# Retention and SwiGLU on one core: four edits to the order and placement of small work in the first batch and at the end

## The chip, the cores and the metric

The kernel runs on one NeuronCore of a Trainium2 chip. Its engines work in parallel, each through its own queue in order: TensorE (PE in the profile; its weight loads are listed apart as PEld), VectorE (DVE), ScalarE (ACT), GpSimd (POOL) and SyncE (SP), which here only issues DMAs. They meet through semaphores. The metric is the device time of one execution in microseconds (us).

## The reference

Eight batches of eight heads go through retention (attention with a decay instead of a softmax); the result, reordered to 4608 tokens of 512 values, goes through a SwiGLU feed-forward block.

```python
# q, k, v: (8, 8, 576, 64) float32; gamma one value per head
scores = scale * np.matmul(q, k.transpose(0, 1, 3, 2))
ret = scores * Dmat          # Dmat[h, i, j] = gamma[h] ** (i - j) for i >= j, else 0
attn = np.matmul(ret, v)
x = attn.transpose(0, 2, 1, 3).reshape(4608, 512)
g = x @ w_gate               # w_gate, w_val: (512, 1536)
val = x @ w_val
out = (g * sigmoid(g) * val) @ w_out      # w_out: (1536, 512)
```

## The kernel before, in words

The tokens are taken in five tiles: tile 0 of 512 tokens, and tiles 1 to 4 of 1024. Everything stays in SBUF; four PSUM banks, `bankA`, `bankB`, `bankC` and `bankE`, take the large matmuls in turn, and `inner` and `outer` hold the retention's.

**Retention.** Heads go in pairs, four pairs per batch. `tick(t)` runs three pairs in different phases at once: it loads and transposes pair t, computes scores and chunk states of pair t-1, and finishes pair t-2, whose values lie in `outer` (matmuls L531, L554, L558) and are copied with their decay into `x` by `to_x` (L646, L622). The next pair's L531 can begin only when those copies have read `outer`. The masks and scans between (L579 to L601) are VectorE's, copies and scalings mostly ScalarE's; from batch 1 on, q and k are transposed by VectorE (L489, into `qT` and `kT`).

**Weights.** The weights come from DRAM in half-blocks. `split(j)` (L404, L405, on ScalarE) takes a half-block's bits apart, and `rounding(j)` (L418, L419, on VectorE) makes the rounded float32 weight of it and calls the next `split`. Roundings 0 to 3 are the gate and value weights of the first two blocks of hidden columns, which `up0` (L747) multiplies in tile 0.

**Tile 0** is multiplied as it stands, `up0` and `down0`. **Tiles 1 to 4** use a bilinear scheme with 26 block products where a plain product has 32. The hidden columns are three quads of 512. For each quad, `up_step` runs 26 steps (the table `UP`); each step adds up a left operand from blocks of the weights and a right operand from blocks of `x`, multiplies them (L972, eight matmuls of 128x256), and adds its result into partial sums. `down_step` does the same 26 times per tile over all three quads (table `DOWN`, L1015, twelve matmuls). A row of `UP` has: the place of its bank in the rotation and whether its product starts a new sum; the slot of the `x` operand and the sums for it; the slot of the weight operand and the sums for it; and what is done with the product. Rows of importance here (steps 0-based):

```python
"3= | 12:  | 11: sub 8 11 6 | copy 6",                                  # step 3
"1= | 4: sub 13 0 2 | 10: nad 11 11 0 | add 2 b 2, neg 12 2",           # step 5
"0+ | 21: add 18 18 7 | 7: nad 9 1 3 | add 2 b 2, sub 4 4 2, add 5 5 4",# step 15
"1+ | 22:  | 8: sub 11 1 10 | add 2 b 2, neg 13 2",                     # step 16
"3= | 18: sub 23 1 3, sub 24 5 23 | 0: nad 6 6 12 | add 6 b 6",         # step 17
"0= | 7:  | 9: add 2 2 4 | add 1 b 1, add 3 b 3, neg 15 1, neg 3 3, add 6 6 3, neg 2 6",  # step 18
"2+ | 24: sub 1 1 5 | 11: sub 12 0 12 | add 3 b 3",                     # step 19
"2+ | 23: sub 25 7 24 | 12: nad 3 3 10 | add 7 b 4, out 1 7",           # step 22
```

In the last column `b` is the bank, numbers are partial sums ("parts", 128x512), `copy` is ScalarE's (L912), and `out` and `neg` end in a SiLU on ScalarE (L990) and a product of it with the value half (L993, L996, L997), which is put off by a step. In the weights' column, `nad d a b` is d = -(a + b): ScalarE negates a into d (L942), then GpSimd subtracts b (L943). Other weight sums are GpSimd's (L781).

In **tile 1** (`busy` in the code, the "first batch" of the change's name; 175.7 to 329.7 us of the span for its up-projection) the weight sums are made for the first time, in place, and each operand is stored to DRAM (L976, issued on ScalarE's queue); tiles 2 to 4 fetch them back (L876). A slot may be overwritten only when its matmul has read it and its store has landed. VectorE does the `x` sums and all sums of `reads` (L915) in this tile; in the others, GpSimd does those sums of `reads` that don't read a bank.

**The order of the work** is written out by hand: inside the manual schedule each engine runs its instructions in the order in which the program emits them. In `up_step`, that is: `x` sums, weight sums with their negations, the matmuls, the store of the weight operand, `reads`, and pieces of retention work (`part_on`) between. Results leave tile by tile: `down_step`'s `result` stores 256 tokens by 256 columns in one DMA (L1024) on SP.

Of the kernel before, what the change touches and what calls it, by code (L numbers as in the profile page):

```python
# [17 lines left out]
ALU = mybir.AluOpType  # L18
# [136 lines left out]
def kernel(  # L155
# [32 lines left out]
    nc = tc.nc  # L188
# [4 lines left out]
    P = 128  # L193
    HP = H // 2
# [7 lines left out]
    TB = TW // 4  # L202
# [4 lines left out]
    starts = list(range(T0 - TW, NT, TW))  # L207
# [465 lines left out]
    def tick(t, lo=HP, hi=NP, spread=False, then=None):  # L673
        go_on(len(pieces))
        if hi == HP:

            if lo <= t - 1 < hi:
                scores(t - 1, True)
                new_states(t - 1)
                pieces.extend(masked(t - 1))  # L680
                go_on(3)
            if lo <= t - 2 < hi:
                own_values(t - 2)
            for f in transposes(t) if lo <= t < hi else ():
                f()
            if t + 1 == HP:
                split(0)
                rounding(0)
            if lo <= t - 2 < hi:
                earlier_values(t - 2)  # L690
                to_x(t - 2)[0]()
            return
        if lo <= t - 2 < hi:
            own_values(t - 2)
        if lo <= t - 1 < hi:
            new_states(t - 1)
        if lo <= t - 2 < hi:
            earlier_values(t - 2)
        if lo <= t - 1 < hi:
            scores(t - 1, t - 2 < lo)  # L700
        if lo <= t - 1 < hi and whole(t - 2) and not whole(t - 1):
            decay(slice(0, H), slice(0, H), half[1])
        copies, *masks = masked(t - 1) if lo <= t - 1 < hi else (lambda: None,)
        keys, *new = transposes(t) if lo <= t < hi else (lambda: None,)
        outputs = to_x(t - 2)[0] if lo <= t - 2 < hi else lambda: None
        late = needed(1) - 4 <= t < needed(1) - 2 or light(t - 2)
        if late and masks:
            own, (pairs, odd, evens) = masks
            pieces.extend([lambda: (copies(), outputs(), own()), [pairs, odd, lambda: (evens(), keys())]])
        elif late:  # L710
            pieces.append(lambda: (copies(), outputs(), keys()))
        else:
            pieces.extend([lambda: (copies(), keys()), outputs])
            pieces.extend(masks)
        if then and new:
            pieces.extend(new[:-1])
            pieces.append(lambda: (new[-1](), then()))
        else:
            pieces.extend(new)
            pieces.extend([then] if then else [])  # L720
        if not spread:
            go_on(len(pieces))
# [176 lines left out]

    products = []  # L900

    def reads(ops, bank, busy, result):

        at = lambda a: bank if a == "b" else part[int(a)]
        old = len(products)
        for op in ops:
            if op[0] in ("copy", "add", "sub"):
                while any(a == op[1] for a, _ in products):
                    products.pop(0)[1]()
                    old -= 1  # L910
            if op[0] == "copy":
                nc.scalar.copy(out=at(op[1]), in_=bank)  # L912
            elif op[0] in ("add", "sub"):
                eng = nc.vector if "b" in op or busy else nc.gpsimd
                eng.tensor_tensor(out=at(op[1]), in0=at(op[2]), in1=at(op[3]),  # L915
                                  op=ALU.add if op[0] == "add" else ALU.subtract)
            else:
                product = result(int(op[1]), at(op[2]), op[0] == "neg", op[2] == "b" or busy)
                if product and op[2] == "b":
                    product()  # L920
                elif product:
                    products.append((op[2], product))
        for _ in range(old):
            products.pop(0)[1]()
# [5 lines left out]
    def x_sums(n, lo, hi, vector):  # L930
        for op in x_ops[lo:hi]:
            add(nc.vector if vector or op[0] == "nad" else nc.gpsimd, op, x_view(n))

    def w_sums(qd, i):
        view = up_view(qd)
        for op in up[i][5]:
            if op[0] == "nad":

                dst, a, b = [view(int(s)) for s in op[1:]]
                if op[3] == op[1]:  # L940
                    a, b = b, a
                nc.scalar.mul(out=dst, in_=a, mul=-1.0)  # L942
                nc.gpsimd.tensor_tensor(out=dst, in0=dst, in1=b, op=ALU.subtract)  # L943
            else:
                add(nc.gpsimd, op, view)
# [10 lines left out]
    def up_step(n, qd, i):  # L956
# [18 lines left out]
        if busy:  # L975
            nc.scalar.dma_start(out=up_ops[qd][i].rearrange("p (g x) -> p g x", g=2), in_=w)  # L976
            if i in (20, 23) and qd + 1 < NQ:
                first_sums(qd + 1, *((0, 2) if i == 20 else (2, 4)))
            if i == 24 and qd + 1 < NQ:
                w_sums(qd + 1, 1)  # L980
            if qd + 1 == NQ:
                for _ in range({21: 3, 22: 2, N - 1: 3}.get(i, 0)):
                    fetch()
        else:
            fetch()
# [10 lines left out]
                return lambda: nc.vector.tensor_tensor(out=dst, in0=src[:, TB : 2 * TB], in1=s, op=ALU.mult)  # L996
            nc.gpsimd.tensor_tensor(out=dst, in0=src[:, TB : 2 * TB], in1=s, op=ALU.mult)  # L997

        reads(ops, b, busy, result)
        if qd + 1 == NQ and i + 1 == N:  # L1000
            while products:
                products.pop(0)[1]()
# [3 lines left out]
    def down_step(n, i):  # L1006
        label, opens, slot, hops, ops = down[i]
        for op in hops:
            add(nc.gpsimd if i % 3 == 1 and op[0] != "nad" else nc.vector, op, hid_view)
        w = operand().rearrange("p (q x) -> p q x", q=NQ)  # L1010
        lhs = hid_view(slot)
        b = bank(label, i == 0)
        for qd in range(NQ):
            for m in range(2):
                nc.tensor.matmul(b[:, m * TB : (m + 1) * TB], lhs[:, qd, ts(m, P)], w[:, qd],  # L1015
                                 start=(opens and qd == 0 and m == 0), stop=(qd == NQ - 1), skip_group_check=True)
        fetch()

        def result(o, src, negative, vector):
            if negative:  # L1020
                nc.scalar.mul(out=src, in_=src, mul=-1.0)
            d, t = divmod(o, 4)
            rows = starts[n] + t * TB
            nc.sync.dma_start(out=out[rows : rows + TB, d * TB : (d + 1) * TB].rearrange("(m p) d -> p m d", p=P),  # L1024
                              in_=src.rearrange("p (m d) -> p m d", m=2))

        reads(ops, b, False, result)
        at = 2 * (i - (N - 1 - X_FIRST // 2))
        if 0 <= at < X_FIRST and n + 1 < NTILE:
            x_sums(n + 1, at, at + 2, True)  # L1030
        go_on(3)
# [10 lines left out]
    for t in range(HP + 2):  # L1042
        tick(t, 0, HP)

        if t == 3:
            load(HP)
        for j in {3: (1,), 4: (2, 3), 5: (4, 5)}.get(t, ()):
            rounding(j)
        for f in range(2):
            if t > 3:  # L1050
# [41 lines left out]
    for m, f in enumerate(down_order):  # L1092
# [6 lines left out]
            first_sums(0, 0, 1)  # L1099
        if m == 8:  # L1100
            first_sums(0, 1, 4)
            w_sums(0, 1)
        if m > 8:
            x_sums(1, 3 * (m - 9), min(3 * (m - 8), X_FIRST), True)
# [64 lines left out]
```

## Time and profile before

| | |
|---|---|
| Median of three runs | 1051.49 us (1051.44 to 1051.83) |
| Profiled execution | 1051.82 us |
| Its span, first to last instruction | 1050.1 us |
| TensorE busy | 1025.6 us, 98% |
| VectorE busy | 660.9 us, 63% |
| GpSimd busy | 393.1 us, 37% |
| ScalarE busy | 294.1 us, 28% |
| VectorE busy from 190 to 330 us | 107.84 of 140 us |
| GpSimd busy from 190 to 330 us | 82.97 of 140 us |
| ScalarE busy from 190 to 330 us | 55.21 of 140 us |

The profile is of one execution; times in its timelines count from the start of the span. A line of a timeline has the start, the duration, the engine, the line of the kernel, the operation, what it writes and reads, the shape, how often it came in a row, and in brackets how long the engine had been idle before it and what ended that. In the table of waits a line has the waiting engine with what it writes and its line, then the releaser, the total in us, the number of waits and the longest. A matmul that starts afresh after a wait is listed somewhat longer than one in a running stream. A sum that reads two operands in SBUF and one that reads a bank have the same line (L915) and differ by what stands after the arrow.

### The profile page before, as it was taken

How to read it: one execution, taken by the hardware profiler on the slowest of the kernel's cores; microseconds unless marked ns; L12 is line 12 of the kernel's file. 1: busy time of each engine (PE TensorE's matmuls, PEld its weight loads, DVE VectorE, ACT ScalarE, POOL GpSimd, SP SyncE). 2: the span in 40 equal slices, each digit the busy share in tenths (PEclk: the TensorE clock that was granted, in tenths of full speed). 3: DMA queues.
4: the chain of work that ended last, by engine and by line, in shares of the span. 5: the costliest groups of instructions: out<-in, count | busy, mean ns of one | idle time of the engine just before them, and what ended most of it. 6: DMA issues, size and time to landing. Idle time of an engine off the chain costs nothing.

```text
span 1050.1 us, 21509 instructions
## 1 busy us (share of the span) xinstructions
PE 1025.6 (98%) x8448; PEld 840.9 (80%) x8448; DVE 660.9 (63%) x1071; ACT 294.1 (28%) x646; POOL 393.1 (37%) x338
## 2 busy tenths in 40 slices
PE   6999999999899999999999999999999999999998
PEld 5444555888787888888888888888888888888887
DVE  5578878778779767554467787526376645344644
ACT  4376433242533322132322102223120022231110
POOL 2002367656365016622124048312250483222505
PEclk9999999999999999999999999999999999999999
DMA  9999768776678788755676777545554565555553
GB/s 243 246 281 278 183 193 271 197 202 183 173 201 228 234 192 261 198 147 172 185 203 160 229 176 226 152 141 151 152 180 137 155 195 156 151 152 161 180 162 98
DMA packets 310363, 199.09 MB, mean 190 GB/s; under 512 B 220152, under 2 KB 254968, under 8 KB 310264
## 3 DMA queue, kind: packets, MB, share of 16 engines
q1 hardware_dynamic: 279128, 161.65, 57.0%
q10 hardware_dynamic: 31136, 36.08, 10.3%
q8 instruction: 67, 1.10, 0.4%
q14 instruction: 32, 0.26, 0.1%
HBM read 157.56 MB, written 40.11 MB: 188 GB/s over the span
## 4 chain that ended last, share of the span: by engine, by line
PE 75%; DVE 5%; issue 1%; ACT 1%; DMA 1%; ACTq 0%; POOL 0%; DVEq 0%; SPq 0%
PE bankC L972 12%; PE bankE L972 12%; PE bankA L972 11%; PE bankB L972 11%; PE bankA L1015 6%; PE bankB L1015 6%; PE bankC L1015 6%; PE bankE L1015 6%; DVE rest L915 2%; PE outer L531 1%; DVE arena L993 1%; PE inner L572 1%; PE outer L558 1%; PE inner L542 1%; DVE rest L781 0%
## 5 line engine op out<-in xcount | busy, mean ns | idle before, releaser
L915 POOL TENSOR_TENSOR rest<-rest 128x512 f32<-128x512 f32 x56 | 79.4, 1423 | 293.1 <-DVE rest L915 274.6
L990 ACT ACTIVATE io<-rest 128x256 f32<-128x256 f32 x180 | 75.0, 417 | 338.2 <-DVE rest L915 289.8
L972 PE MATMUL bankC<-rest,arena 128*128 128x256 f32 x544 | 129.1, 380 | 0.5 <-DVE rest L915 0.5
L972 PE MATMUL bankA<-rest,arena 128*128 128x256 f32 x544 | 128.8, 380 | 0.0
L781 POOL TENSOR_TENSOR arena<-arena 128x512 f32<-128x512 f32 (+1 forms) x72 | 115.4, 1617 | 29.0 <-DMA up<-arena 20.9
L972 PE MATMUL bankE<-rest,arena 128*128 128x256 f32 x512 | 121.4, 380 | 2.5 <-DVE rest L915 2.5
L972 PE MATMUL bankB<-rest,arena 128*128 128x256 f32 x512 | 121.4, 380 | 0.8 <-POOL arena L943 0.8
L972 PEld LDWEIGHTS bankC<-rest,arena 128*128 128x128 f32 x544 | 102.9, 190 | 15.3 <-issue 0.9
L972 PEld LDWEIGHTS bankA<-rest,arena 128*128 128x128 f32 x544 | 103.1, 190 | 14.8 <-issue 0.8
L997 POOL TENSOR_TENSOR arena<-rest,io 128x256 f32<-128x256 f32 x72 | 51.9, 725 | 166.9 <-ACT io L990 166.9
L972 PEld LDWEIGHTS bankE<-rest,arena 128*128 128x128 f32 x512 | 96.9, 190 | 16.4 <-issue 2.3
L972 PEld LDWEIGHTS bankB<-rest,arena 128*128 128x128 f32 x512 | 97.0, 190 | 14.7 <-POOL arena L943 1.6
L781 POOL TENSOR_TENSOR rest<-rest 128x256 f32<-128x256 f32 (+1 forms) x66 | 67.5, 1044 | 102.2 <-DVE rest L419 61.7
L915 DVE TENSOR_TENSOR rest<-bankC,rest 128x512 f32<-128x512 f32 x72 | 48.7, 685 | 64.4 <-PE bankC L972 43.6
L915 DVE TENSOR_TENSOR rest<-bankB,rest 128x512 f32<-128x512 f32 x72 | 48.8, 686 | 63.7 <-PE bankB L972 44.8
L915 DVE TENSOR_TENSOR rest<-bankE,rest 128x512 f32<-128x512 f32 x72 | 48.8, 685 | 63.2 <-PE bankE L972 46.2
L915 DVE TENSOR_TENSOR rest<-bankA,rest 128x512 f32<-128x512 f32 x72 | 48.8, 686 | 62.8 <-PE bankA L972 45.5
L993 DVE SCALAR_TENSOR_TENSOR arena<-rest,io 128x256 f32<-128x256 f32 x84 | 58.5, 699 | 10.9 <-ACT io L990 10.9
L1015 PE MATMUL bankA<-arena 128*128 128x256 f32 x252 | 58.0, 380 | 1.3 <-DVE arena L781 1.3
L1015 PE MATMUL bankB<-arena 128*128 128x256 f32 x252 | 58.4, 382 | 0.0
L1015 PE MATMUL bankC<-arena 128*128 128x256 f32 x252 | 58.1, 380 | 0.0
L1015 PE MATMUL bankE<-arena 128*128 128x256 f32 x252 | 57.9, 379 | 0.0
(188 smaller groups left out, 1632.3 us busy)
## 6 DMA issues: line engine op xcount, KB each, us to landing
arena<-up SPq DMA_DIRECT2D x234, 256.0 KB, 2.7
arena<-dn SPq DMA_DIRECT2D x104, 384.0 KB, 3.6
up<-arena ACTq DMA_DIRECT2D x78, 256.0 KB, 3.2
dn<-rest SPq DMA_DIRECT2D x78, 128.0 KB, 1.8
out_dram<-rest SPq DMA_DIRECT2D x32, 256.0 KB
qk<-in_q_dram SPq DMA_DIRECT2D x108, 72.0 KB, 2.5
qk<-in_k_dram SPq DMA_DIRECT2D x108, 72.0 KB, 2.6
rest<-in_moe_w_out_dram ACTq DMA_DIRECT2D x6, 1024.0 KB
```

The lines of the kernel that those rows point to most:

```text
L531: m = nc.tensor.matmul(value(i, hl, c), s["v"][rows, at], ret[rows, c % 2 if whole(i) else hl, c // 2], start=start, stop=start, skip_grou ...
L542: nc.tensor.matmul(z[half[hl], r, c], s["kn"][chunk(i, hl, 2 * c + r, i < HP)], s["v"][rows, at], start=True, stop=True, skip_group_check= ...
L558: nc.tensor.matmul(xr[half[hl]] if c + 1 == NC else value(i, hl, c), state[half[hl], c, :], s["qT"][half[hl], column(i, hl, c)], start=Fal ...
L572: nc.tensor.matmul(sc[chunk(i, hl, 2 * c + r)[0], r if whole(i) else hl, c], kT[half[hl], at], qT[half[hl], at], start=True, stop=True, sk ...
L781: eng.tensor_tensor(out=dst, in0=srcs[0], in1=srcs[1], op=ALU.add if op[0] == "add" else ALU.subtract)
L915: eng.tensor_tensor(out=at(op[1]), in0=at(op[2]), in1=at(op[3]), op=ALU.add if op[0] == "add" else ALU.subtract)
L972: m = nc.tensor.matmul(b[:, gv * TB : (gv + 1) * TB], w[:, gv, ts(c, P)], rhs[:, c, :], start=(opens and gv == 0 and c == 0), stop=(c == 1 ...
L990: nc.scalar.activation(out=s, in_=src[:, 0:TB], func=AF.Silu, scale=-1.0 if negative else 1.0)
L993: return lambda: nc.vector.scalar_tensor_tensor(out=dst, in0=src[:, TB : 2 * TB], scalar=-1.0, in1=s, op0=ALU.mult, op1=ALU.mult)
L997: nc.gpsimd.tensor_tensor(out=dst, in0=src[:, TB : 2 * TB], in1=s, op=ALU.mult)
L1015: nc.tensor.matmul(b[:, m * TB : (m + 1) * TB], lhs[:, qd, ts(m, P)], w[:, qd], start=(opens and qd == 0 and m == 0), stop=(qd == NQ - 1), ...
```

## The change

There are four edits.

1. At the start, `tick(3)` emits `rounding(0)` after the output copies of pair 1 instead of before them, and `tick(4)` emits `rounding(2)` and `rounding(3)` before the output copies of pair 2; they were emitted after that tick.
2. In tile 1 the negation of a step's `nad` is emitted a step earlier by a new function `negated`: after the store of the step before and ahead of that step's `reads`.
3. In tile 1, from step 14 on, sums of `reads` that read no bank go to GpSimd instead of VectorE (`spread`).
4. The very last sum of the kernel and its store are split into two halves of 128 tokens, the second stored through ScalarE's queue.

```diff
 def tick(...)
             if t + 1 == HP:
                 split(0)
-                rounding(0)
             if lo <= t - 2 < hi:
                 earlier_values(t - 2)
+                if t == HP:
+                    rounding(2)
+                    rounding(3)
                 to_x(t - 2)[0]()
+            if t + 1 == HP:
+                rounding(0)
             return
...
-    def reads(ops, bank, busy, result):
+    def reads(ops, bank, busy, result, spread=False):
...
-                eng = nc.vector if "b" in op or busy else nc.gpsimd
+                eng = nc.vector if "b" in op or (busy and not spread) else nc.gpsimd
...
+    def negated(qd, i):
+
+        view = up_view(qd)
+        for op in up[i][5]:
+            if op[0] == "nad":
+                nc.scalar.mul(out=view(int(op[1])), in_=view(int(op[3] if op[3] == op[1] else op[2])), mul=-1.0)
+
     def w_sums(qd, i):
...
-                nc.scalar.mul(out=dst, in_=a, mul=-1.0)
                 nc.gpsimd.tensor_tensor(out=dst, in0=dst, in1=b, op=ALU.subtract)
...
             if i == 24 and qd + 1 < NQ:
+                negated(qd + 1, 1)
                 w_sums(qd + 1, 1)
+            if 0 < i < N - 1:
+                negated(qd, i + 1)
...
-        reads(ops, b, busy, result)
+        reads(ops, b, busy, result, i > N // 2)
...
+        if n + 1 == NTILE and i + 1 == N:
+            _, o, a = ops.pop()
+            d, t = divmod(int(o), 4)
+            at, rows = part[int(a)], starts[n] + t * TB
+            assert ops == [["add", a, "b", a]]
+            for m, queue in enumerate((nc.sync, nc.scalar)):
+                nc.vector.tensor_tensor(out=at[:, ts(m, TB)], in0=b[:, ts(m, TB)], in1=at[:, ts(m, TB)], op=ALU.add)
+                queue.dma_start(out=out[rows + m * P : rows + (m + 1) * P, d * TB : (d + 1) * TB], in_=at[:, ts(m, TB)])
+            return
...
-        for j in {3: (1,), 4: (2, 3), 5: (4, 5)}.get(t, ()):
+        for j in {3: (1,), 5: (4, 5)}.get(t, ()):
             rounding(j)
...
             first_sums(0, 1, 4)
+            negated(0, 1)
             w_sums(0, 1)
```

## The prediction

> **What bounds the kernel now.** I read the engine table first, then TensorE's waits, then the timelines around those waits.
>
> ```profile
> PE 1025.6 (98%) x8448; PEld 840.9 (80%) x8448; DVE 660.9 (63%) x1071; ACT 294.1 (28%) x646; POOL 393.1 (37%) x338
> ```
>
> TensorE (PE) works through 98% of the span: 24.5 us of idle is all that a change off TensorE can win, and only where it ends a wait. The waits, one line each (waiter, releaser, us, times, longest):
>
> ```profile
> PE outer L531 <- DVE rest L622: 2.6, 2, 2.3
> PE bankE L972 <- DVE rest L915: 2.5, 2, 1.9
> PE outer L566 <- DVE kT L489: 1.6, 1, 1.6
> PE bankB L972 <- POOL arena L943: 0.8, 2, 0.5
> PE bankC L972 <- DVE rest L915: 0.5, 1, 0.5
> ```
>
> All lie before 330 us, where the start (to 42 us) and tile 1's up-projection (175.7 to 329.7 us, three quads of 26 steps of 1.73 us) are. In the start, VectorE's timeline (start, duration, engine, line) and TensorE's show the 2.3 us wait:
>
> ```profile
> 22.70 0.43 DVE L418 TENSOR_SCALAR arena<-rest 128x512 int32<-128x512 int32 x1 [0.75 <-ACT rest L404]
> 23.29 0.69 DVE L419 CUSTOM_DVE_ANT_0 arena<-arena,rest 128x1024 uint16<-128x1024 uint16 x1 [0.16 <-ACT rest L405]
> ...
> 24.03 1.28 DVE L622 TENSOR_TENSOR rest<-outer,tab 128x256 f32<-128x256 f32 x3
> 25.70 0.46 PE L531 MATMUL outer<-ret,v 64*64 64x64 f32 x16 [2.29 <-DVE rest L622]
> ```
>
> Rounding 0 (L418, L419) stands in VectorE's queue ahead of the output copies (L622) that free PSUM's `outer` for TensorE.
>
> In the up-projection VectorE is the engine that runs late. Quad 1, steps 15 to 22, timelines of VectorE, GpSimd (POOL), ScalarE (ACT) and TensorE:
>
> ```profile
> 254.05 2.38 DVE L915 TENSOR_TENSOR rest<-rest 128x512 f32<-128x512 f32 x2
> 262.26 1.68 DVE L915 TENSOR_TENSOR rest<-rest 128x512 f32<-128x512 f32 x1
> 263.87 2.90 DVE L993 SCALAR_TENSOR_TENSOR arena<-rest,io 128x256 f32<-128x256 f32 x2
> 266.87 0.69 DVE L915 TENSOR_TENSOR rest<-bankE,rest 128x512 f32<-128x512 f32 x1
> 254.52 1.36 POOL L943 TENSOR_TENSOR arena<-arena 128x512 f32<-128x512 f32 x1 [6.30 <-ACT arena L942]
> 260.71 5.77 POOL L781 TENSOR_TENSOR arena<-arena 128x512 f32<-128x512 f32 x4
> 253.81 0.63 ACT L942 ACTIVATE arena<-arena 128x512 f32<-128x512 f32 x1 [0.60 <-DMA up<-arena]
> 267.70 1.96 PE L972 MATMUL bankE<-rest,arena 128*128 128x256 f32 x8 [1.93 <-DVE rest L915]
> ```
>
> The first two lines are the three sums that this change moves; step 22 waits 1.93 us for bank E, which the fourth line frees.
>
> [...]these 512-wide sums take 0.69 us alone (233.48) and 1.68 us beside GpSimd, while sums with a PSUM input stay at 0.69 us.[...]
>
> **The change part by part.**
>
> *Start: 1.4 us.* Rounding 0 goes behind the copies of head pair 1, roundings 2 and 3 ahead of those of pair 2; ScalarE's order stays. The copies need pair 1's matmuls, whose last (L558) end near 22.4, and VectorE is free at 21.96: they run 22.4 to 23.8 instead of 23.9 to 25.3. TensorE, ready at 23.4, goes on near 24.2 instead of 25.70: 1.5 us. Next late: rounding 0 now 23.8 to 25.1, for a matmul due at 25.7; rounding 1 to 26.3, due 27.5; masks 26.3 to 28.9; rounding 2 to 30.1, while bank C's matmul comes due at 29.2. It waited 0.85 us at 31.76 and starts near 30.3: 1.45 us. Rounding 3 ends at 31.3, due 32.1; copies of pair 2 end at 32.7, needed at 33.9. From 42 to 164 us TensorE has no wait. The weight roundings lead it by 5 us at 53 us, and the long run of stores on SP (69 from 131.50) begins behind loads of k and v whose buffers TensorE frees, so it shifts along. I take 1.4.
>
> *Negations: nothing by themselves, 0.3 us in quad 2.* Six weight sums per quad need a negation on ScalarE. Two keep their place in ScalarE's order (those of steps 1 and 7); those of steps 5, 15, 17 and 22 move ahead of the SiLU of the step before, which waited for VectorE. No instruction is added; one is 0.61 us. GpSimd's sums of steps 5, 17 and 22 are released some 1.5 to 4 us earlier. That ends the 0.3 us at 190.00 (step 8), but step 9 then waits for VectorE (0.56 us at 192.56), so nothing is won. In quad 2, step 25 waits 0.28 us for the sum at 326.56, released by a negation at 325.87; a step ahead it is done by 324: with its restart 0.3 us. What is queued behind: step 15's negation waits for the store of step 13 (landed 253.8), and now SiLU 14 stands behind it, 252.80 becoming some 254.4. VectorE's product of it comes only after step 15's sums, and its wait is under 1 us, where 2.4 us of sums are gone. Without that cover every us of late landing is a us of VectorE.
>
> *Sums to GpSimd: 1.2 us.* The queues show three per quad, nine in all, not four: two at step 15, one at step 18. VectorE loses 2.38 + 1.68 us in quad 1. GpSimd gains 3 x 1.27 = 3.8 us per quad, and its order ties it: step 16's `add 2 b 2` must wait until GpSimd has read part 2, and step 19's `add 3 b 3` until it has read part 3. Quad 1: sum of step 15's weights 254.5 to 255.8, VectorE's product to 256.15, the two moved sums to 258.7, then two weight sums and a VectorE product of 0.35 to 261.6 (step 20 needs the second at 262.16), `add 2 2 4` to 262.9, product to 263.25, moved sum to 264.5, product to 264.85, and bank E is read by 265.5 instead of 267.5. Step 21 ends at 265.6: the 1.93 us wait is gone. But GpSimd, idle from 266.5 to 271.9 before, now still has three sums to do until 270.3, and they cost VectorE some 0.6 us at a product and 0.9 at the small scans (L596). So `kT` (L489), for which TensorE waited 1.58 us until 278.49, comes only 1.1 us earlier, and of the 1.93 I keep 1.1. Quad 0: the same sum, from 205.74: `sub`, `add`, two weight sums to 212.7, where step 20 needs it at 212.0 and got it at 212.45; bank C is free near 216.3 to 216.6, where it was 216.65: 0.1 us. Quad 2: bank A at 321.1 to 322.4 against 322.2: 0, from -0.15 to 0.15.
>
> *Last sum in halves: 0.4 us.* The last matmul ends at 1045.85, the sum at 1046.64, the last store is issued at 1046.67, moves its 256 KB from about 1047.4 to 1048.3, and the span ends at 1050.1. Two halves of 0.41 and 0.33 us end at the same 1046.7, and ScalarE, idle, issues the second. It moves 128 KB, half of 0.9 us, so 0.4 us. The rest is fixed: [...]here 1.8 us follow the last bytes. Bounds 0 and 0.6.
>
> Sum: 1.4 + 0.3 + 1.1 + 0.1 + 0.4 = 3.3 us. The profiled execution took 1051.82 us (span 1050.1 and 1.7 around it), so 1048.5; from the median of 1051.49 it is 1048.2 us, 0.31% less. Bounds of the unknowns: start 0 to 1.6, quads -2 to 3.4, tail 0 to 0.6.
>
> **The rivals.** *A, everything arrives:* GpSimd slots its sums in without holding VectorE, `kT` keeps the full 2.0 us, quad 0 gains 0.5, and the 1.76 us pause at 337.43, which no wait explains, falls away in part. 3.3 + 0.9 + 0.4 + 0.9 = 5.5 us: 1046.0. For it: GpSimd is 37% busy. Against: it and VectorE meet in just this stretch.
>
> *B, the start's gain is eaten:* TensorE waits 0.64 us at 164.70 for VectorE (L601), which was itself held by stores `dn<-rest` on SP. If these keep their time, TensorE arriving 1.4 us earlier waits 1.4 more: 1.9 us remain, 1049.6. Against it: the run of stores begins at a buffer that TensorE frees.
>
> *C, `kT`[...] takes back all of quad 1:* 2.2 us remain, 1049.3.
>
> *D, slower: GpSimd sets the pace.* Between step 15 and bank E's release stand seven GpSimd operations in line. Each costs d; I used 1.27, while L781's mean in this stretch is 1.41 and single ones reach 1.8. At 1.8 quad 0's step 20 starts at 215.5 and step 22 at 220.5 (3.7 us late), quad 1's step 22 1.2 late, quad 2's 1.1: 6 us lost against 1.8 kept at both ends, 1055.7. The three quads lose about 1.4 us per 0.1 us of d, so the whole breaks even near 1.5 us and is measurably slower from 1.65. Against it: the stretching is mostly the VectorE operations that I have counted singly.
>
> **How the numbers follow.** The forecast 0.58 (1046.7 to 1049.4), A 0.12, B 0.13, C 0.10, D 0.07. A measurement of this kernel can tell about 0.2%, 2.1 us: faster is below 1049.4. The forecast and A count there but for 0.05, and 0.05 of B and C: 0.70 faster. D is slower in 0.05, 0.25 remain. The range 1045.4 to 1051.0 leaves out D and the outer ends of A and B.
>
> **What would show it.** In the changed kernel TensorE's first large wait for L622 should be under 0.9 us, and the matmul at 27.21 start near 25.7. Quad 1's step 22 should wait under 0.3 us; TensorE should wait longer for `kT`, some 2.5 us. On GpSimd nine more sums of 1.2 to 1.5 us appear, and its idle time behind negations, 42.8 us in this stretch, falls. From the last matmul to the end it should be 3.9 us, not 4.3. Wrong would be: waits of TensorE for weight sums at steps 20, SiLU 14 more than 2 us later, or a wait near 164 us above 1.5 us.

## The result, and the profile after

The changed kernel takes 1048.13 us (median of 20 runs, 1043.79 to 1056.52); the kernel before, on the same chip, 1053.49 us (median of 20, 1049.35 to 1058.48). The ratio is 0.9957, with a 95% interval from 0.9941 to 0.9973: 0.43% faster, some 4.5 us (the two medians lie 5.4 us apart), where 3.3 us (0.31%) were forecast. The profiled execution took 1046.57 us, its span 1044.8 us, against 1051.82 and 1050.1 before. Single runs spread over 9 us (before) and 13 us (after), so one profile of each is not enough; second ones come below.

First the engine table of the changed kernel's page, and the line of its DMA queues that will matter:

```profile
PE 1025.3 (98%) x8448; PEld 842.7 (81%) x8448; DVE 648.1 (62%) x1063; ACT 295.2 (28%) x646; POOL 401.8 (38%) x347
...
q8 instruction: 67, 1.10, 0.4%
```

Queue q8 carries instructions: 67 packets, 1.10 MB. GpSimd (POOL) has nine instructions more, three per quad as forecast. TensorE's busy time has not moved. Its waits (waiter, releaser, us, times, longest):

```profile
PE outer L531 <- DVE arena L418: 2.4, 1, 2.4
PE inner L572 <- issue: 2.3, 1, 2.3
...
PE outer L566 <- DVE kT L489: 1.1, 1, 1.1
PE bankE L982 <- DVE rest L919: 1.0, 1, 1.0
```

The waits of the up-projection for bank E, bank B and bank C are gone but for 1.0 us, the one for `kT` is shorter rather than longer, and the first large wait, for L531, is as long as before: 2.4 for 2.3 us. (Lines have moved: L972 is now L982, L915 is L919, L942 and L943 are L943 and L953, L781 is L785, L993 to L997 are L1006 to L1010, L1015 is L1028.) Timelines of VectorE and TensorE in the start of the changed kernel:

```profile
22.53 1.28 DVE L622 TENSOR_TENSOR rest<-outer,tab 128x256 f32<-128x256 f32 x3
23.84 0.43 DVE L418 TENSOR_SCALAR arena<-rest 128x512 int32<-128x512 int32 x1
26.12 1.50 PE L531 MATMUL outer<-ret,v 64*64 64x64 f32 x32 [2.38 <-DVE arena L418]
```

VectorE does what was forecast to 0.1 us: the copies (L622) end at 23.81 us. TensorE still starts L531 at 26.12 and not near 24.2, and then runs it at half clock (granted clock 0.50 from 26.0 to 29.4 us; 32 matmuls in 1.50 us, before in 1.01).

Quad 1 of the up-projection, steps 15 to 22, timelines of VectorE, GpSimd and TensorE:

```profile
254.62 0.69 DVE L919 TENSOR_TENSOR rest<-bankB,rest 128x512 f32<-128x512 f32 x1 [1.17 <-POOL rest L919]
262.04 0.69 DVE L919 TENSOR_TENSOR rest<-bankE,rest 128x512 f32<-128x512 f32 x1
253.21 2.74 POOL L919 TENSOR_TENSOR rest<-rest 128x512 f32<-128x512 f32 x2 [0.68 <-DVE rest L919]
260.20 1.42 POOL L919 TENSOR_TENSOR rest<-rest 128x512 f32<-128x512 f32 x1 [0.39 <-DVE rest L919]
263.82 1.89 PE L982 MATMUL bankE<-rest,arena 128*128 128x256 f32 x8
```

The three sums run on GpSimd at 1.37 to 1.42 us each; VectorE waits 1.17 us for one of them, as the prediction's order of parts 2 and 3 demanded; step 22 has no wait, since VectorE has read bank E at 262.7, 1.1 us before it.

**By stretches**, from the first matmul of the up-projection, and with it the second profile of either kernel (from the experiments below), and the start reordered alone, whose up-projection is the old one:

| us | before | before, 2nd | start alone | after | after, 2nd |
|---|---|---|---|---|---|
| L531 near 25 us starts at | 25.70 | 25.33 | 28.71 | 26.12 | 25.66 |
| up-projection begins at | 175.7 | 175.6 | 178.0 | 175.6 | 173.6 |
| quad 0, to quad 1's first step | 48.1 | 49.9 | 47.4 | 46.4 | 46.5 |
| quad 1, to its step 25 | 49.5 | 49.5 | 48.6 | 47.0 | 47.3 |
| its step 25 to quad 2's first step, with the wait for `kT` | 6.0 | 6.0 | 6.0 | 5.4 | 6.0 |
| quad 2, to its step 25 | 48.7 | 48.7 | 48.6 | 48.2 | 49.9 |
| last matmul's end to the span's end | 4.26 | 4.26 | 4.26 | 3.82 | 3.81 |

The gain is in the quads, 5.2 us in the first pair of profiles, and at the very end, 0.4 us. (In the last column TensorE ran at half clock for 3.4 us from 273.7 us on, which costs 1.7 us there.) At the start L531 is no earlier. What stands between it and the up-projection differs by 2 us between the two profiles of the changed kernel, one of which has 3.4 us of half clock there; what the start is worth has to come from the times below.

### The profile page after: what moved, and what is told of

It reads as the page before. It is cut to its first block, busy times and chain, and to the rows that moved or that the text cites. A ratio compares the mean times of both kernels' runs of the same rounds, so it can differ in the third digit from the quotient of the medians.

```text
span 1044.8 us, 21507 instructions
## 1 busy us (share of the span) xinstructions
PE 1025.3 (98%) x8448; PEld 842.7 (81%) x8448; DVE 648.1 (62%) x1063; ACT 295.2 (28%) x646; POOL 401.8 (38%) x347
## 4 chain that ended last, share of the span: by engine, by line
PE 79%; DVE 2%; issue 1%; ACT 0%; DMA 0%; ACTq 0%; DVEq 0%
PE bankC L982 13%; PE bankE L982 12%; PE bankA L982 12%; PE bankB L982 12%; PE bankA L1028 6%; PE bankB L1028 6%; PE bankC L1028 6%; PE bankE L1028 6%; PE outer L531 1%; PE inner L572 1%; PE outer L558 1%; PE inner L542 1%; DVE rest L919 1%; DVE rest L785 0%; PE outer L566 0%
## 5 line engine op out<-in xcount | busy, mean ns | idle before, releaser
L919 POOL TENSOR_TENSOR rest<-rest 128x512 f32<-128x512 f32 x65 | 91.7, 1416 | 298.4 <-DVE rest L919 276.8
L982 PE MATMUL bankC<-rest,arena 128*128 128x256 f32 x544 | 129.0, 380 | 0.0
L982 PE MATMUL bankA<-rest,arena 128*128 128x256 f32 x544 | 128.7, 379 | 0.0
L785 POOL TENSOR_TENSOR arena<-arena 128x512 f32<-128x512 f32 (+1 forms) x72 | 111.8, 1565 | 39.9 <-DMA up<-arena 26.5
L982 PE MATMUL bankE<-rest,arena 128*128 128x256 f32 x512 | 121.4, 380 | 1.0 <-DVE rest L919 1.0
L982 PE MATMUL bankB<-rest,arena 128*128 128x256 f32 x512 | 121.2, 379 | 0.0
L1010 POOL TENSOR_TENSOR arena<-rest,io 128x256 f32<-128x256 f32 x72 | 52.1, 729 | 166.7 <-ACT io L1003 166.7
L982 PEld LDWEIGHTS bankA<-rest,arena 128*128 128x128 f32 x544 | 103.2, 190 | 14.5 <-issue 0.5
L982 PEld LDWEIGHTS bankC<-rest,arena 128*128 128x128 f32 x544 | 102.9, 190 | 14.5 <-POOL arena L785 0.3
L982 PEld LDWEIGHTS bankE<-rest,arena 128*128 128x128 f32 x512 | 97.0, 190 | 14.6 <-DVE rest L919 1.4
L982 PEld LDWEIGHTS bankB<-rest,arena 128*128 128x128 f32 x512 | 97.0, 190 | 13.3
L785 POOL TENSOR_TENSOR rest<-rest 128x256 f32<-128x256 f32 (+1 forms) x66 | 67.8, 1048 | 102.0 <-DVE rest L419 62.0
L919 DVE TENSOR_TENSOR rest<-bankB,rest 128x512 f32<-128x512 f32 x72 | 48.9, 687 | 67.4 <-PE bankB L982 49.3
L919 DVE TENSOR_TENSOR rest<-bankC,rest 128x512 f32<-128x512 f32 x72 | 48.8, 685 | 66.5 <-PE bankC L982 45.6
L919 DVE TENSOR_TENSOR rest<-bankA,rest 128x512 f32<-128x512 f32 x72 | 48.8, 686 | 62.9 <-PE bankA L982 45.5
L919 DVE TENSOR_TENSOR rest<-bankE,rest 128x512 f32<-128x512 f32 x71 | 48.1, 686 | 61.8 <-PE bankE L982 46.6
L1006 DVE SCALAR_TENSOR_TENSOR arena<-rest,io 128x256 f32<-128x256 f32 x84 | 57.2, 682 | 11.3 <-ACT io L1003 11.3
L1028 PE MATMUL bankA<-arena 128*128 128x256 f32 x252 | 58.0, 380 | 1.3 <-DVE arena L785 1.3
L1028 PE MATMUL bankB<-arena 128*128 128x256 f32 x252 | 58.5, 381 | 0.0
L1028 PE MATMUL bankC<-arena 128*128 128x256 f32 x252 | 58.1, 380 | 0.0
L1028 PE MATMUL bankE<-arena 128*128 128x256 f32 x252 | 57.9, 379 | 0.0
```

Source lines behind the costliest of these rows:

```text
L785: eng.tensor_tensor(out=dst, in0=srcs[0], in1=srcs[1], op=ALU.add if op[0] == "add" else ALU.subtract)
L982: m = nc.tensor.matmul(b[:, gv * TB : (gv + 1) * TB], w[:, gv, ts(c, P)], rhs[:, c, :], start=(opens and gv == 0 and c == 0), stop=(c == 1 ...
L1006: return lambda: nc.vector.scalar_tensor_tensor(out=dst, in0=src[:, TB : 2 * TB], scalar=-1.0, in1=s, op0=ALU.mult, op1=ALU.mult)
```

## The experiments

Each ratio is to runs of the kernel before taken beside it, with a 95% interval. The diffs are shortened; "..." marks what is left out.

**The start alone.** If the copies are early and L531 is not, it may wait for something else: its own instructions. The changed kernel's DMA table has a queue of the kind "instruction", q8, with 67 packets of 16 KB. Its trace lists 17298 instructions of TensorE's (8448 matmuls, 8448 weight loads, and 402 that wait, branch or the like), and the pauses below stand a multiple of 256 of them apart; 17298 are 67.6 times 256. So I read a packet as a block of 256 of TensorE's instructions. Only one to four of the 67 or 68 packets in a profile have such a pause behind them.

```diff
             if t + 1 == HP:
                 split(0)
-                rounding(0)
             if lo <= t - 2 < hi:
                 earlier_values(t - 2)
+                if t == HP:
+                    rounding(2)
+                    rounding(3)
                 to_x(t - 2)[0]()
+            if t + 1 == HP:
+                rounding(0)
...
-        for j in {3: (1,), 4: (2, 3), 5: (4, 5)}.get(t, ()):
+        for j in {3: (1,), 5: (4, 5)}.get(t, ()):
```

> The kernel before with the reordering of the start alone (rounding 0 behind the output copies of head pair 1, roundings 2 and 3 ahead of those of pair 2). Theory P, the prediction's step: the copies end near 23.8 us, TensorE goes on near 24.2 us and the kernel gains 1.4 us, ratio 0.9987. Rival F, the fetch: what TensorE waits for at 25.70 us is the next block of its own instructions. The 16 KB instruction packet of the kernel before starts at 23.42 us and ends at 24.34, that of the changed kernel ends at 24.55, and TensorE went on 1.36 and 1.57 us later. Then the copies are early and TensorE still starts its L531 between 25.5 and 26.2 us; only bank C's 0.85 us at 31.76 us can go, 0 to 0.9 us in all, ratio 0.9992 to 1.0000.

Measured: ratio 1.0003 (0.9990 to 1.0016); 1054.18 us. Timelines of VectorE and TensorE:

```profile
25.26 1.28 DVE L622 TENSOR_TENSOR rest<-outer,tab 128x256 f32<-128x256 f32 x3
23.82 0.39 PE L476 MATMUL bankC<-ident,rest 64*64 64x64 f32 x6 [1.29 <-issue]
28.71 1.01 PE L531 MATMUL outer<-ret,v 64*64 64x64 f32 x32 [2.57 <-DVE arena L418]
```

The copies end at 26.54, and L531 starts 2.2 us later. The wait in front of it is put down to L418, the last thing that VectorE finished by then, but the program has L531 wait for the copies alone. The instruction packet ended at 27.31, and L531 starts 1.40 us after it. At 23.82 there is a pause with no releaser at all ("issue"), and it too ends 1.53 us after the end of a packet.

**All but the start.** The changed kernel with the diff above taken back.

```diff
...
-            if t + 1 == HP:
-                rounding(0)
...
```

> The changed kernel with the start put back to its old order, all else kept. Theory P (the start is worth 1.4 us of the whole): 1.4 us slower than the changed kernel, so about 3 us faster than before, ratio 0.997. Rival F (the start brought nothing, all the gain is in the up-projection and the tail): as fast as the changed kernel, some 4 to 5 us faster than before, ratio 0.9955 to 0.996, with a TensorE wait near 25.7 us as long as before and bank C's wait of 0.85 us back.

Measured: ratio 0.9961 (0.9950 to 0.9973), against 0.9957 for the whole change: the start is worth nothing that can be measured. In its profile TensorE's L531 starts at 24.88, 1.64 us after its packet's end, and only 0.05 us behind the copies: here they ended the wait. The profile also has a wait of 3.10 us in quad 0, and shows what can follow one (timelines of VectorE and TensorE):

```profile
23.54 1.28 DVE L622 TENSOR_TENSOR rest<-outer,tab 128x256 f32<-128x256 f32 x3
24.88 0.71 PE L531 MATMUL outer<-ret,v 64*64 64x64 f32 x16 [1.95 <-DVE rest L622]
...
192.61 3.75 PE L978 MATMUL bankA<-rest,arena 128*128 128x256 f32 x8 [3.10 <-DVE rest L915]
```

Eight matmuls that take 1.99 us elsewhere take 3.75: the granted clock was one half from 191.8 us, 0.8 us before the wait ended, to 198.6.

**The moved sums alone, and the negations alone.**

```diff
-                eng = nc.vector if "b" in op or busy else nc.gpsimd
+                eng = nc.vector if "b" in op or (busy and not spread) else nc.gpsimd
...
```

> The kernel before with the three sums per quad moved to GpSimd alone, the negations in their old place. Theory P: 1.2 us gained; step 22 of quad 1 waits under 0.3 us where it waited 1.93; the wait for kT grows to some 2.5 us. Rival Q (the negations carry the sums: without them GpSimd's weight sums stand behind a negation and behind the moved sums): steps 20 wait 0.5 us or more for a weight sum in quads 0 and 1, and the gain is under 1 us. Rival R (the sums are worth more than I counted, because VectorE is the late engine through all of the stretch): lead of 3 us or more over the kernel before at 330 us, kT's wait no longer than 1.6 us, ratio 0.997.

Measured: ratio 0.9951 (0.9935 to 0.9967), 1048.78 us. Quad 1 takes 47.0 us, quad 2 48.2, as in the changed kernel; the wait for `kT` is 1.53 us. Quad 0's step 19 waits 1.60 us for a weight sum: GpSimd does it at 215.99 us, behind the two moved sums, which stood behind the sum of a negation at 211.48. That is rival Q's mechanism, a step earlier than Q had it, but not the small gain that Q expected. Rival R, "worth more than I counted", is nearest.

```diff
...
-                nc.scalar.mul(out=dst, in_=a, mul=-1.0)
                 nc.gpsimd.tensor_tensor(out=dst, in0=dst, in1=b, op=ALU.subtract)
...
+            if 0 < i < N - 1:
+                negated(qd, i + 1)
...
```

> The kernel before with the negations a step ahead alone. Theory P: 0.3 us, all of it at step 25 of quad 2; the 0.30 us at 190.00 only moves to step 9. Rival Q (step 20's weight sums are released by them): the waits of 0.51 us at 212.53 (quad 0, step 20) and 0.28 at quad 2's step 25 go as well, but step 22 of quad 1 still waits 1.9 us for bank E: 0.8 us in all. Neither has more than 1 us, ratio 0.999 to 1.000.

Measured: ratio 0.9956 (0.9940 to 0.9972), 1050.9 us. That is as much as the whole change gains, from an edit that was priced at 0.3 us; both expectations missed. Its profile, of one of its slowest executions (1056.31 us), shows no gain (2.51 us and 2.15 us of wait at steps 22), so this kernel was run again, and beside it the kernel before, unchanged.

> The kernel before, unchanged, once more: a second profile, and how far one kernel's times lie from another draw of its own. Ratio 1.000, interval some 0.1% each side. Theory S (the profiles differ from run to run in the start and in TensorE's clock, the rest of the kernel repeats): from the first step of the up-projection to its last 150.5 to 152.5 us as in the first profile (152.2), with waits for VectorE at quad 0's steps 8 or 9 and 22, quad 1's step 22 and for kT; and the pauses at 21.09 and 339.19 us again at the same instructions. Rival: the waits for VectorE move by more than 2 us between two profiles of one kernel, and a single profile can't carry a sum of 3 us.

Measured: ratio 1.0003 (0.9989 to 1.0016), so a kernel compared with itself gives 1. But the rival has half of the truth: quad 0 took 49.9 us where it had taken 48.1, with waits at steps 7 and 8 (0.78 and 1.04 us) that the first profile lacks or has shorter. Quad 1, `kT`, quad 2 and the pause in L572 (1.76 us again, three matmuls before its end) repeat to 0.1 us. Its L531 starts 0.07 us behind the copies.

> The kernel with the negations alone, a second time: its times said 0.44% faster, its profile showed VectorE later than before at step 22 of quads 0 and 1 (2.51 and 2.15 us), in an execution among its slowest. Theory N (the negations alone are worth 4 us): ratio 0.9956 again, and a profile in which the up-projection takes under 150 us and step 22 of quad 1 waits under 1 us. Rival P (they are worth 0.3 us, and the first time was luck of the draw): ratio 0.998 to 1.001, waits at steps 22 as long as before.

Measured: ratio 0.9958 (0.9942 to 0.9973): theory N on the time. Timelines of VectorE and GpSimd in quad 1, first of the kernel before (second profile; quad 1 begins at 225.5 us):

```profile
258.12 1.49 DVE L996 TENSOR_TENSOR arena<-rest,io 128x256 f32<-128x256 f32 x1
261.28 1.52 DVE L993 SCALAR_TENSOR_TENSOR arena<-rest,io 128x256 f32<-128x256 f32 x1
264.03 1.68 DVE L915 TENSOR_TENSOR rest<-rest 128x512 f32<-128x512 f32 x1
268.64 0.69 DVE L915 TENSOR_TENSOR rest<-bankE,rest 128x512 f32<-128x512 f32 x1
255.91 1.73 POOL L943 TENSOR_TENSOR arena<-arena 128x512 f32<-128x512 f32 x1 [5.93 <-ACT arena L942]
262.48 5.77 POOL L781 TENSOR_TENSOR arena<-arena 128x512 f32<-128x512 f32 x4
```

and then of the kernel with the negations alone (quad 1 begins at 223.5 us):

```profile
256.61 1.49 DVE L1005 TENSOR_TENSOR arena<-rest,io 128x256 f32<-128x256 f32 x1
259.24 0.41 DVE L1002 SCALAR_TENSOR_TENSOR arena<-rest,io 128x256 f32<-128x256 f32 x1
261.68 0.69 DVE L915 TENSOR_TENSOR rest<-rest 128x512 f32<-128x512 f32 x1
265.31 0.69 DVE L915 TENSOR_TENSOR rest<-bankE,rest 128x512 f32<-128x512 f32 x1
251.94 1.28 POOL L949 TENSOR_TENSOR arena<-arena 128x512 f32<-128x512 f32 x1 [3.92 <-ACT arena L939]
256.09 3.13 POOL L781 TENSOR_TENSOR arena<-arena 128x512 f32<-128x512 f32 x2
```

Counted from the beginning of the quad, step 15's weight sum starts at 28.4 us for 30.4. GpSimd is through the next ones earlier, and is idle from 259.2 to 262.0 us, where VectorE does a product and begins the third sum: 0.41 and 0.69 us, for 1.52 and 1.68 beside GpSimd. The bank is read 41.8 us into the quad instead of 43.1, and TensorE's wait at step 22 is 0.65 us for 1.93. No instruction of VectorE was taken away; two of the late ones got shorter. This is one profile of two: the first one of this kernel, in which step 22 waited 2.15 us, does not show it, so the times carry the gain, and the next experiment the place.

**Which negations.**

```diff
...
-            if 0 < i < N - 1:
+            if i + 1 in (15, 17):          # the other kernel: (5, 7, 22)
                 negated(qd, i + 1)
...
```

Against the kernel with all negations ahead, each of these two leaves the negations that it doesn't name in their old place.

> The kernel before with the negations of steps 15 and 17 alone a step ahead; those of steps 5, 7 and 22 keep their place. Theory L (the negations pay because GpSimd's sums of steps 15 and 17 run earlier and no longer beside VectorE's two-input operations: with all negations ahead the sum of step 15's weights began 28.4 us into quad 1 where it began at 30.4, and VectorE's third sum took 0.69 us for 1.68, its product at step 17 0.41 for 1.52): quad 1 up to its step 25 takes 48.5 us or less where it took 49.4, step 22 waits under 1 us, and half or more of the 0.42% is there: ratio 0.9955 to 0.998. Rival W (it is the waits for the weight sums of steps 8 and 20 that the other negations end): ratio 0.999 to 1.000 here.

Measured: ratio 0.9973 (0.9956 to 0.9990). Quad 1 takes 47.4 us, step 22 has no wait: theory L, as far as quad 1 goes.

> The kernel before with the negations of steps 5, 7 and 22 alone a step ahead; those of steps 15 and 17 keep their place. Theory L: quad 1 as before (step 22 waits 1.5 to 2 us), gain under half, ratio 0.998 to 1.000. Rival W: no wait for a weight sum at steps 8 and 20 of quad 0, 0.3 to 1.6 us there, and most of the gain here, ratio 0.9955 to 0.9975.

Measured: ratio 0.9989 (0.9975 to 1.0003). Quad 1 takes 48.7 us, with 1.33 us of wait at step 22; no weight sum is waited for in quad 0. The two parts add up to 0.38%, near the 0.42 to 0.44% of all negations. The greater part seems to come from steps 15 and 17, but the intervals overlap. Quad 0 stays a matter of chance: VectorE's timeline of the kernel with steps 15 and 17 shows two products that took 0.75 us with all negations ahead (at 214.83 us there):

```profile
215.54 2.90 DVE L1005 SCALAR_TENSOR_TENSOR arena<-rest,io 128x256 f32<-128x256 f32 x2
```

GpSimd's next sums, which wait for a store to land, began at 215.00 us here, 0.5 us ahead of the products, and at 215.40 in the other, 0.6 us behind the start of the first. Step 22 of quad 0 waited 3.58 us in this profile, and its eight matmuls then took 3.49 us from their start to the next step's, for 1.73 a step later.

**Moving the blocks of instructions.** If TensorE stands still at the end of a block, the place must move when instructions are put ahead of it.

```diff
         if i < HP:
+            for _ in range(8 if i == 0 else 0):          # the other kernel: 32
+                nc.tensor.matmul(bankC[half[0], 0:L], ident[half[0], half[0]], ident[half[0], half[0]],
+                                 start=True, stop=True, skip_group_check=True)
```

> The changed kernel with 8 extra 64x64 matmuls of the identity ahead of TensorE's first transposes, where it waits for q (from 1.5 to 4.2 us it has nothing to do): their output is overwritten, the result unchanged. They are 32 instructions more on TensorE (a weight load and a matmul, twice each), so every 256th instruction comes 32 earlier in the program. Theory F (TensorE stands where its next 16 KB block of instructions[...] hasn't come): the pause of 2.31 us in L572 at 334.37, three matmuls before its end, moves 16 matmuls ahead and shrinks to 0 to 0.5 us, since the block before it then begins in the longer matmuls and is fetched some 2 us earlier. The start: the pause before L531 at 26.12 moves into L542 (half of its 32 matmuls before, half behind it) and ends 0 to 1 us earlier. 2 us faster than the changed kernel if no other boundary falls into a run of small matmuls, so ratio 0.9935 to 0.9945. Rival (the pause belongs to that place: a semaphore or a bank): it stays at the same matmul with 1.7 to 2.3 us, ratio 0.9955.

Measured: ratio 0.9929 (0.9908 to 0.9950). TensorE's timelines of this kernel (L572 is L575 here, L542 is L545, L531 is L534):

```profile
23.14 0.46 PE L545 MATMUL inner<-v,rest 64*64 64x64 f32 x14 [0.53 <-POOL rest L507]
24.94 0.68 PE L545 MATMUL inner<-v,rest 64*64 64x64 f32 x16 [1.34 <-issue]
25.38 1.47 PE L534 MATMUL outer<-ret,v 64*64 64x64 f32 x32
...
331.49 0.63 PE L575 MATMUL inner<-qT,kT 64*64 64x64 f32 x30
332.05 2.21 PE L1031 MATMUL bankC<-arena 128*128 128x256 f32 x9
```

and of the changed kernel at the second place:

```profile
331.43 0.63 PE L572 MATMUL inner<-qT,kT 64*64 64x64 f32 x27
334.37 0.33 PE L572 MATMUL inner<-qT,kT 64*64 64x64 f32 x3 [2.31 <-issue]
```

32 instructions are 16 matmuls with their weight loads, and the pause at the start now stands 16 matmuls ahead of L531's first, with "issue" beside it: in the changed kernel it was no wait for VectorE. The 2.31 us in L572 are gone. L531 starts at 25.38, 0.3 to 0.7 us earlier than in the two profiles of the changed kernel.

> The same with 32 extra matmuls, 128 instructions, half a block. They take some 2.3 us at half clock, in TensorE's idle time to 4.2 us. Theory F: no pause at 334 us; at the start the blocks begin earlier, TensorE pauses in L558 or L572 near 18 us and in L572 near 22 us instead, and L531 starts near 24.2 to 25 us, 1 to 2 us earlier than 26.12, which is the prediction's 1.4 us for the start, then due. 2 to 4 us faster than the changed kernel where no new pause arises, ratio 0.992 to 0.994. Rival (a fixed place): pause at 334 us and start as before, ratio 0.9955.[...]

Measured: ratio 1.0008 (0.9992 to 1.0025). The pauses moved: into L572 (L575 here) at 22.27 and 26.80, 1.17 and 1.11 us, and none is left near 334 us. But the 32 matmuls took 7.08 us, not 2.3, so the first scores began at 11.60 us for 7.95; a block now ends in L558 (L561 here) at 32.00 with 2.72 us, and one at 522.75 with 1.11. The theory's places were right, the gain was not: the four pauses add up to 6.1 us, where the changed kernel's two have 4.7, and the late beginning comes on top.

> The changed kernel with 8 extra small matmuls ahead of TensorE's first transposes, once more, beside the changed kernel itself on the same chip. Theory F: no pause of 1.7 to 2.3 us in L572 after the up-projection, a pause of 1 to 1.5 us in the middle of L542 near 23.6 us; 2 to 3 us faster than the changed kernel, ratio to the kernel before 0.993.

> The changed kernel itself once more, for a second profile. From the first step of the up-projection to its last 147 to 148.5 us where the kernel before had 152.2 and 154.1; no gain at the start, TensorE's L531 between 25.5 and 26.3 us unless the matmuls ahead of it come later; the pause in L572 after the up-projection again three matmuls before its end, between 0.3 and 2.4 us as the fetch falls; 3.8 us from the last matmul to the end; ratio 0.9955 to 0.9965.

Measured: 0.9898 (0.9879 to 0.9916), 1043.27 us, for the one; 0.9938 (0.9913 to 0.9962), 1047.97 us, for the other. With eight matmuls that compute nothing the kernel is faster than both kernels of this case; what it gains over the changed one, some 4 us here and 3 by the first run, is more than the pause. The clock has a part in that. In the second profile of the changed kernel the pause in L572 (2.03 us) was followed by 3.4 us of half clock, which costs 1.7 us more; and the granted clock of each run, taken as lost time, is 0.8 us on the mean of these five runs and 2.3 us on the mean of the six beside them. With so few runs this is a hint.

**All pauses together.** The start and end of each instruction packet are in the trace. In 14 profiles TensorE's pauses with no releaser, and its L531 near 25 us where it is not among them, number 33. In four of them (the second profile of the kernel before, all but the start, the negations alone for the first time, steps 15 and 17) L531 starts 0.05 to 0.07 us behind the last copy, so the copies ended these waits. The other 29 end 1.2 to 1.6 us after the end of the last packet, whatever VectorE had done by then. In the kernel before L531 is one of those: it starts 0.38 us behind the copies and 1.36 behind the packet.

The places tell the same. Counted over TensorE's instructions in the trace, in order of their start, each of the 33 stands at a number that leaves 194 (twice 193) when it is divided by 256: the pauses lie whole blocks of 256 apart, in kernels with and without extra matmuls.

## Why the prediction was right in sum and wrong in its parts

The forecast was 3.3 us, the measurement 4.5 (2.8 to 6.2). The sum was nearly right, but in part by luck: one of its terms gave nothing that could be measured, two were far too small, and those two overlap.

- **Start, 1.4 us: wrong.** Alone it measured 0.3 us lost (from 1.1 gained to 1.7 lost). The failing step is "TensorE, ready at 23.4, goes on near 24.2 instead of 25.70". VectorE's queue was worked out rightly, but the reading "PE L531 <- DVE L622" was taken as a cause. In the profile before, the copies end at 25.32, and the packet of instructions at 24.34; with the 1.2 to 1.6 us of the 29 cases its block was usable at 25.5 to 25.9 (an estimate): two releasers at nearly the same moment, of which the later, the block, is not named. In the four profiles where the copies came last, they did so by 0.5 us at most (an estimate: their L531 against the end of the packet and 1.4 us, the middle of the 29 cases). There were two signs. Pauses by "issue" stood in L476 (0.38 us) and L572 (1.76 us); the second I called unexplained and left, the first I did not mention. And L531 came 0.38 us behind the copies, which I took for the usual delay ("23.8" to "near 24.2"); where the copies do end the wait, it is 0.05 to 0.07 us. The end of bank C's wait, the other half of this term, did come: the 0.85 us at 31.76 are in no profile with the new order. But they are missing from four with the old one too.
- **Negations, "nothing by themselves, 0.3 us in quad 2": wrong by more than ten times**, 4.4 and 4.6 us alone in two measurements. Quad 2 gave 0.5 us for the 0.3 stated; but it takes the same 48.2 us with the sums alone, and with the negations of steps 15 and 17 alone, so the one negation named is not what it takes. The failing step is the one that looked only for waits for weight sums which an earlier negation would end. An earlier negation also moves GpSimd's whole run of sums, and with it the time at which VectorE is stretched. The stretching was in the prediction (0.69 us alone, 1.68 beside GpSimd), used for the sums that move and not for those that stay.
- **Sums, 1.2 us: the mechanism was right, the size was not.** Alone they gave 5.2 us (3.5 to 6.9). Step 22 of quad 1 is without a wait, as stated, and quad 1 up to its step 25 takes 47.0 us for 49.5. What I took off again was the error: `kT` was to come only 1.1 us earlier because GpSimd's late sums would hold VectorE. In the changed kernel TensorE is 4.8 us earlier at `kT` and waits 1.1 us (1.7 in the second profile), not 2.5: VectorE itself waits 0.99 us for ScalarE at 270.91, just before `kT`, so it is no longer the engine that runs late. Quad 0, put at 0.1 us, gave 1.7 us between the first profiles: the waits at steps 8, 20 and 22 went (1.35 us), step 9's grew by 0.45, and the rest is not in waits. Not all of that is the sums': alone they have 47.6 us there, the negations 46.1 in one profile and 51.7 in the other.
- **The two are not a sum.** Alone the sums gave 0.49% and the negations 0.42 and 0.44%; together with the tail's part they gave 0.39% (all but the start). In quad 1 the sums alone reach 47.0 us, the negations alone 48.5, both 47.0. So both seem to take the same lateness from VectorE, one by shortening its operations, the other by taking three away. I added them as if their waits were different ones.
- **Tail, 0.4 us: right**: 3.81 to 3.82 us from the last matmul to the end in the six profiles with the halves, 4.26 to 4.28 in seven of the eight without (3.97 in one). The part behind the stores' last bytes, put at 1.8 us and as fixed, is 1.7 us in the first profile of the kernel before and 1.5 in that of the changed one.
- **Of the rivals**, A (everything arrives, 5.5 us) came nearer in the quads (2.8 us, for 5.2 in the first profiles) and had the start wrong; its pause at 337.43 us did not shrink but lasted 2.31 us. B, which ate the start's gain, had no gain to eat; the wait of 0.64 us at 164.70 is absent from both profiles after. C, which took back all of quad 1, did not come. D needed 1.5 us for a GpSimd operation, for the 1.27 that L943 takes at 205.74 before; the three sums took 1.37 to 1.42, so its point was near but not reached.
- **The queue**: three sums per quad, as read from the order of the instructions, not the four of the change's name.

One term was not in the sum: what a wait costs beyond its length. The profiles have stretches of 3.4 or 6.8 us in which the granted clock is one half, and some lie at the end of a wait. Of 26 waits of 1.4 us or more after 100 us, in 14 profiles, 11 have such a stretch, which begins between 0.8 us before their end and 1.7 us after it: all five of 2.5 us or more, 6 of 21 shorter ones. Each 3.4 us of it costs some 1.7 us (an estimate: in one of them eight matmuls took 3.75 us for 1.99).

But the gain is not made of this. The mean granted clock is on record for every run but those of the kernel before in the first comparison. One minus it, times the span, is the time lost to the clock: 3.0 us on the mean of the 20 runs of the changed kernel, and 3.3 us on the mean of the 127 runs of the kernel before that were taken beside the experiments. That is 0.3 us of the 4.5, with an uncertainty of some 0.9. The negations alone lose 3.4 and 3.2 us, the sums alone 2.3.

What is open: why the packet for L572 sets out within 0.3 us of the moment at which TensorE goes into the block before in two profiles (the sums alone, the negations again), where the pause is 0.34 us, and 1.1 to 2.3 us later in nine, where it is 1.7 to 2.3; and which of the chances in quad 0 (waits of 2.5 to 3.6 us at step 7 or 22 in five of 14 profiles) a single landing decides.

## What to carry to other kernels

Before a gain is read off a wait, look for a second releaser that ends at the same moment: a pause by "issue" at the same instruction in every profile, and an instruction packet that ended just before (1.2 to 1.6 us) meant here that the engine had no instructions, and reordering VectorE's work brought nothing (ratio 1.0003 for the start alone). A start that comes later behind its named releaser than elsewhere (0.38 us for 0.05 to 0.07 here) is a sign of it. Where an operation of one engine takes longer beside those of another (0.69 us for a sum of VectorE's alone, 1.68 beside GpSimd), price a moved operation by what will run beside it afterwards, on both sides; two edits that relieve the same late engine are alternatives, not terms of a sum. Take a second profile of the kernel before wherever a forecast rests on waits under 2 us.

## What the runs showed of the hardware that was not expected

- TensorE can run out of instructions. In 14 profiles 29 of its pauses, 0.3 to 2.7 us long, stand whole blocks of 256 instructions apart and end 1.2 to 1.6 us after the end of a 16 KB packet of instructions, which takes 0.9 to 1.9 us (the first profiles of the two kernels). All stand where a block ends at or within 64x64 matmuls, of which about 130, with their weight loads, take 2.2 us. Eight matmuls put ahead of the first moved these ends by 32 instructions; that kernel is 3 to 4 us faster.
- A 64x64 matmul of the identity at the beginning takes 0.11 us from start to start (64 in 7.08 us; in the kernel with eight such matmuls ahead 16 are listed with 1.97 us), five times as long as the 64x64 matmuls of L542 later (32 in 0.65 us) and three times as long as those of L572 at 8 us (28 in 1.04 us). Why is not shown.
- At the end of 11 of 26 waits of 1.4 us and more stands a stretch of half clock of 3.4 or 6.8 us; in one of them eight matmuls took 3.75 us for 1.99.
